# The order of gate and weight conversion in a two-layer feed-forward stage

## The chip, the cores and the metric

One core of a Trainium2 chip. The metric is the device time in microseconds (us) of one launch. "PE" is TensorE (matmuls; "PEld" its weight loads), "DVE" VectorE, "ACT" ScalarE, "POOL" GpSimd, "SP" the queue that issues the loads from memory.

## What is computed

Attention with a position bias for 2 x 8 heads of 576 tokens, whose output goes as 1152 rows of 512 through two feed-forward layers:

```python
attn_out = _attn_ref(**attn_kwargs)
x = np.ascontiguousarray(attn_out.transpose(0, 2, 1, 3)).reshape(B * S, H * D)
x = _moe_ref(x=x, **moe_kwargs)      # h = x @ w_in; g = h * sigmoid(1.702 h); g @ w_out
return _moe2_ref(x=x, **moe2_kwargs) # h = x @ w_in; g = P(h) / Q(h);          g @ w_out
```

Each layer has 512 inputs, 2048 hidden units and 512 outputs. Its weights `w_in` and `w_out` arrive in double precision.

## The kernel before, in words

**Stages.** Attention comes first, and its last steps overlap the start of the first layer (about 184 us into the span). Then follow the first layer (to about 390 us) and the second (to the end).

**Steps.** The hidden units are cut into 16 tiles of 128 ("f-tiles", `NF`), the 1152 rows into 3 chunks of 384 (`NC`, `CH`). A pair of a chunk and an f-tile is one step `n` of the main loop: 48 steps of the first layer (0 to 47, `N1 = 48`), then 48 of the second. The first layer takes f-tiles 0 to 7 for chunks 0, 1, 2 (steps 0 to 23), then f-tiles 8 to 15 for chunks 2, 1, 0 (steps 24 to 47). The second takes chunks 2, 1, 0 with all 16 f-tiles each. The first three steps are issued beside the end of attention, so the main loop begins with step 3.

**What a step issues**, each engine working through its own queue in the order of issue:

- PE, "hidden" (`hidden`, L476; matmuls at L483): 12 matmuls `w_in` times x into a PSUM tile `hps`. There are two such tiles, so hidden of step n needs the gate of step n-2 to have read its tile.
- The gate of the step before, n-1 (`gelu`, L498): ACT takes the sigmoid of `hps` into `sg` (L501), DVE multiplies `hps` and `sg` (L502), ACT rounds the product into `ghi` (L492), POOL subtracts to get the rest `glo` (L495). In the second layer the gate is `rational` (L509): it is spread over three steps, with ACT (L521 to L529), DVE (L531 to L545) and POOL (L542, L544). Its functions need another table on ACT, loaded once at step 48 (L899).
- PE, "out" (`out1`, L560, matmuls at L564; in the second layer `out2`, L567, at L571): the product of an earlier step (two steps back in the first layer, four in the second) times `w_out`, added up in PSUM. At the end of a run of f-tiles the sums are taken out (L819, L826, L848; the copies `xhi`, `xlo` of L831 and L832 follow one per step).

**Conversions.** A weight tile (`w_in` or `w_out` of one f-tile of one layer) is loaded as raw 64-bit numbers (`raw`, three buffers, L420) and turned into a rounded half and a rest. Conversion `j` does, in this order: on DVE it finishes conversion j-1 (`join`, L461), and begins its own with a shift into `top` (L446) and a merge (L451); on ACT it takes the lower word into `up` (L445), and casts the finished weights j-1 into the tile `w` (L471); POOL subtracts to get the rest of j-1 into `w` (L472); SP issues a load two conversions ahead. One set of 16 tiles `w` serves both layers, so a tile of the second layer can be written only when the first layer's last read of that f-tile is through. Which conversion comes is set by the list `M.order`; when, by the rules at L879 to L892 of the main loop: one per step, a second in the steps of the table `twice`, none before the old weights are freed, and from step 52 on one in every second step, where its DVE parts are put between those of `rational`.

**Order within a step, steps 6 to 48:** hidden, then the first conversion, then the gate, then the second conversion if there is one, then out. (Steps 3 to 5 have the gate ahead of both.)

**Conversions by step before:** one in each of steps 6 to 34; two in step 35; none in steps 36 to 40, since the next tile in the list is f-tile 8, which the first layer still reads; then 1, 1, 1, 2, 2, 2, 1 in steps 41 to 47; one in every even step from 52 to 64; the last `join` in step 66.

Of the kernel before, what the change touches and what calls it, by code (L numbers as in the profile page):

```python
# [17 lines left out]
NF = 16  # L18
# [4 lines left out]
L1, L2 = 2, 4  # L23
# [28 lines left out]
class Attention:  # L52
    def __init__(self, tc, t):
        self.tc, self.nc, self.t = tc, tc.nc, t
# [344 lines left out]
class Moe:  # L399
    def __init__(self, tc, t):  # L400
        self.tc, self.nc, self.t = tc, tc.nc, t
        self.raw, self.tmp, self.up, self.W = {}, {}, {}, {}
        self.hs, self.second = None, False
        self.ready = None
        self.order = [(0, k, o) for k in range(NF) for o in range(2)]
        self.order += [(1, k - L1 * o, o) for k in range(NF + L1) for o in range(2) if 0 <= k - L1 * o < NF]

# [165 lines left out]
def attention_moe_moe(tc, t):  # L575
    nc = tc.nc
    new = tc.alloc_tile_pool
    A, M = Attention(tc, t), Moe(tc, t)
# [33 lines left out]
    o = (1, 0, 3, 2, 5, 4, 7, 11, 6, 9, 8, 10)  # L612
# [42 lines left out]
    n = len(A.steps)  # L655
    nj = [0]

    def conv(now=True):
        M.conv(nj[0])
        nj[0] += 1  # L660
        if now:
            M.split()

    pv, hq, due = [], [], []
    A.pv = pv
    g, nh = {}, 0
    for s in range(n + TLAG + 2):
# [3 lines left out]
        if s < n:  # L671
            hp, b, qc = A.steps[s]
            pb = 2 * hp + b
            i = QORDER.index(qc)
# [77 lines left out]
        if s < n:  # L752
# [3 lines left out]
            if s:  # L756
                h, o, c = A.steps[s - 1]
# [46 lines left out]
    N1 = NC * NF  # L804
# [3 lines left out]
    freed = {k: max(due[n] - L1 for n in range(N1) if seq[n][2] == k) for k in range(NF)}  # L808
    acc, ng, later, hr = {}, len(g), [], []

    twice = (35, 37, 39, 40, 44, 45, 46)
    gq = list(range(N1, len(seq)))
    todo = list(range(len(seq)))

# [14 lines left out]
    def input2_parts():  # L829
        p, hi, lo = later.pop(0)  # L830
        nc.scalar.copy(hi, p)  # L831
        nc.gpsimd.tensor_tensor(out=lo, in0=p, in1=hi.bitcast(F32), op=ALU.subtract)  # L832
# [38 lines left out]
    for n in range(nh, len(seq) + L2):  # L871
        l, c, k = seq[n] if n < len(seq) else (2, 0, 0)
        M.second = l > 0
        if l < 2:
            (hr if l else hq).append(M.hidden(c, k))
        fs = []
        if n < 6:
            g[n - 1] = M.gelu(hq.pop(0))
        for i in range(2):  # L879
            j = nj[0]  # L880
            if j < 33:
                go = i == 0 or n < 6
            elif j < 65:
                go = freed[M.order[j - 1][1]] + L1 * M.order[j - 1][2] < n
                go = go and (n < N1 and (i == 0 or n in twice) or n >= N1 + 4 and n % 2 == 0 and i == 0)
            else:
                go = False
            if go and n >= N1:
                fs = M.convs(j)
                nj[0] += 1  # L890
            elif go:
                conv(False)  # L892
            if n < N1:
                M.split()
            if i == 0 and 6 <= n <= N1:
                g[n - 1] = M.gelu(hq.pop(0))

        if n == N1:
            nc.scalar.activation(out=small[:, 0:1], in_=small[:, 2:3], func=AF.Abs_reciprocal_sqrt)  # L899

        if n == N1 + 3:
            outs(n)
        if hr or n >= len(seq):
            r = M.rational(hr.pop(0) if hr else None, n < N1 + 4, fs)
            if r:
                g[gq.pop(0)] = r
        M.split()
        if later:
            input2_parts()
        if n != N1 + 3:  # L910
            outs(n)
# [74 lines left out]
```

## Time and profile before

| | |
|---|---|
| median of 3 runs | 605.54 us (605.29 to 606.39) |
| the profiled execution | 605.63 us, span 603.5 us |
| PE busy | 570.9 us (95% of the span) |
| ACT busy | 440.2 us (73%) |
| DVE busy | 427.4 us (71%) |
| POOL busy | 392.6 us (65%) |

The span runs from the first to the last instruction of the profiled execution; some 2 us of its time lie around it. The chain that ended last is PE for 63% of the span. Shares of busy time are an average over the stages: to see what a change is worth, one has to look at single steps.

### The profile page before, as it was taken

To read this page: it belongs to the slowest core of one execution; us is meant where nothing else is said; L and a number is where in the kernel's file an instruction comes from. 1 tells how busy PE (TensorE), PEld (TensorE's weight loads), DVE (VectorE), ACT (ScalarE), POOL (GpSimd) and SP (SyncE) were. 2 spreads that over 40 slices of the span, in tenths; PEclk is the share of its full clock that TensorE was granted. 3 is DMA by queue.
4 is the path that set the end of the run, shared out by engine and by line. 5 is a ranking of instruction groups with operands and counts; after the bars stand their busy time and mean duration, and the time that the engine had idled before them with its cause. 6 is when DMAs were issued, how large, how long until landed. Compare 5 with 4: busy or idle time off the path is not lost.

```text
span 603.5 us, 11022 instructions
## 1 busy us (share of the span) xinstructions
PE 570.9 (95%) x3805; PEld 477.7 (79%) x3805; DVE 427.4 (71%) x922; ACT 440.2 (73%) x927; POOL 392.6 (65%) x466
## 2 busy tenths in 40 slices
PE   6977999999889989999999999999999999999997
PEld 2233466666557989999999999988899899898995
DVE  7988756888876886657554527769899666667663
ACT  7977777898886675546454535679999978788783
POOL 5967666777764675546563536849888756566563
PEclk9999999999999999999999999999999999999999
DMA  5788762916314563525443313701210100001001
GB/s 175 209 269 277 225 233 83 317 60 229 113 36 140 175 209 118 163 78 168 138 111 101 105 36 105 210 1 35 72 35 2 52 2 1 1 15 38 2 1 52
DMA packets 23911, 66.25 MB, mean 110 GB/s; under 512 B 2480, under 2 KB 3376, under 8 KB 23856
## 3 DMA queue, kind: packets, MB, share of 16 engines
q1 hardware_dynamic: 23712, 65.43, 34.1%
q8 instruction: 30, 0.49, 0.3%
q14 instruction: 25, 0.20, 0.1%
q10 hardware_dynamic: 144, 0.13, 0.1%
HBM read 52.30 MB, written 13.25 MB: 109 GB/s over the span
## 4 chain that ended last, share of the span: by engine, by line
PE 63%; DVE 12%; ACT 11%; POOL 7%; issue 4%; DMA 3%; ACTq 0%; DVEq 0%; POOLq 0%
PE hps L483 23%; PE acc L564 12%; PE acc L571 11%; PE wide L215 5%; PE xt L370 3%; DVE p L236 3%; DMA bias_all<-st 2%; PE wide L122 2%; POOL ra L544 2%; POOL w L472 2%; DVE tmp L461 2%; PE pt L295 2%; PE pt L332 1%; POOL glo L495 1%; ACT w L471 1%
## 5 line engine op out<-in xcount | busy, mean ns | idle before, releaser
L483 PE MATMUL hps<-xhi,w 128*128 128x384 f32 x768 | 151.3, 338 | 3.4 <-DVE part L545 1.8
L483 PEld LDWEIGHTS hps<-xhi,w 128*128 128x128 f32 x768 | 135.5, 188 | 10.3 <-DVE part L545 3.9
L472 POOL TENSOR_TENSOR w<-tmp,w 128x512 fp32r<-128x512 f32 x64 | 85.9, 1342 | 36.3 <-ACT w L471 30.6
L495 POOL TENSOR_TENSOR glo<-sg,ghi 128x384 fp32r<-128x384 f32 x48 | 49.0, 1020 | 54.2 <-PE acc L564 40.6
L483 PE MATMUL hps<-xlo,w 128*128 128x384 f32 x384 | 82.0, 334 | 0.0
L253 POOL TENSOR_SCALAR p<-p,mn 128x512 f32<-128x512 f32 x72 | 55.4, 780 | 37.7 <-ACT p L240 26.2
L564 PE MATMUL acc<-ghi,w 128*128 128x384 f32 x384 | 78.3, 334 | 0.0
L571 PE MATMUL acc<-w,ghi 128*128 128x512 f32 x288 | 76.0, 393 | 1.1 <-POOL w L472 1.1
L240 ACT ACTIVATE p<-p,mn 128x576 f32<-128x576 f32 x72 | 55.4, 771 | 20.2 <-DVE mn L236 18.3
L483 PEld LDWEIGHTS hps<-xlo,w 128*128 128x128 f32 x384 | 68.0, 188 | 0.0
L564 PEld LDWEIGHTS acc<-ghi,w 128*128 128x128 f32 x384 | 67.6, 188 | 0.0
L542 POOL TENSOR_SCALAR ra<-ra,small 128x384 f32<-128x384 f32 x48 | 28.4, 592 | 53.2 <-ACT ra L527 53.1
L502 DVE TENSOR_TENSOR sg<-hps,sg 128x384 f32<-128x384 f32 x48 | 26.8, 558 | 50.6 <-ACT sg L501 50.6
L571 PEld LDWEIGHTS acc<-w,ghi 128*128 128x128 f32 x288 | 53.3, 188 | 10.0 <-POOL w L472 1.4
L236 DVE CUSTOM_DVE_ANT_0 p<-wide,bt 128x576 f32<-128x576 f32 x72 | 52.3, 750 | 2.3 <-DMA bt<-bias_all 2.1
L492 ACT CAST ghi<-sg 128x384 fp32r<-128x384 f32 x48 | 24.7, 514 | 39.4 <-PE acc L564 21.2
L544 POOL TENSOR_TENSOR ra<-ra,part 128x384 f32<-128x384 f32 x48 | 50.1, 1044 | 4.0
L445 ACT ACTIVATE up<-raw 128x512 int32<-128x512 uint32 x59 | 37.6, 637 | 19.1 <-DVE tmp L461 18.0
L215 PE MATMUL wide<-k,q 64*128 64x288 f32 (+1 forms) x432 | 45.2, 309 | 2.3 <-ACT st L142 2.0
L564 PE MATMUL acc<-glo,w 128*128 128x384 f32 x192 | 45.0, 334 | 0.0
L571 PE MATMUL acc<-w,glo 128*128 128x512 f32 x144 | 42.5, 392 | 0.0
L501 ACT ACTIVATE sg<-hps 128x384 f32<-128x384 f32 x48 | 23.5, 490 | 24.6 <-PE hps L483 24.6
(113 smaller groups left out, 1180.0 us busy)
## 6 DMA issues: line engine op xcount, KB each, us to landing
raw<-win SPq DMA_DIRECT2D x32, 512.0 KB, 3.5
raw<-wout SPq DMA_DIRECT2D x32, 512.0 KB, 3.5
bias_all<-st SPq DMA_DIRECT2D x36, 295.5 KB, 3.9
bt<-bias_all SPq DMA_DIRECT2D x16, 576.0 KB, 6.2
qk<-qk SPq DMA_DIRECT2D x7, 608.0 KB, 6.6
v<-v SPq DMA_DIRECT2D x8, 320.0 KB, 5.0
out<-o SPq DMA_DIRECT2D x8, 256.0 KB, 2.2
bt<-bias_all SPq DMA_DIRECT2D x8, 144.0 KB, 3.3
```

The costliest lines, as they stand in the source:

```text
L215: nc.tensor.matmul(ps[:, half, 0:288], q[p, x, 128 * qc:128 * qc + 128], k[p, y, 288 * half:288 * half + 288], start=(i == 0), stop=(i == ...
L236: nc.vector.tensor_tensor_reduce(out=pv.rearrange("p (x j) -> p x j", x=2), in0=ps[:, :, 0:288], in1=self.bt[qc][:, a, :].rearrange("p (x ...
L240: nc.scalar.activation(out=pv, in_=pv, func=AF.Exp, bias=mn[:, a:a + 1], scale=-1.0, accum_out=mn[:, 2 + a:3 + a])
L253: nc.gpsimd.tensor_scalar(out=p[:, a, 0:512], in0=p[:, a, 0:512], scalar1=r, scalar2=1.0, op0=ALU.mult, op1=ALU.mult)
L445: nc.scalar.activation(out=self.up[j].bitcast(I32), in_=lo, func=AF.Copy, scale=2.0 ** -29)
L472: nc.gpsimd.tensor_tensor(out=w[:, 2 * o + 1, :], in0=val, in1=w[:, 2 * o, :].bitcast(F32), op=ALU.subtract)
L483: nc.tensor.matmul(ps[:, 0:CH], w[:, wi, 128 * d:128 * d + 128], xx[:, d, :], start=(i == 0 and d == 0), stop=(i == 2 and d == 3))
L495: nc.gpsimd.tensor_tensor(out=glo[:], in0=g, in1=ghi[:].bitcast(F32), op=ALU.subtract)
L542: nc.gpsimd.tensor_scalar(out=t0[0][:], in0=t0[0][:], scalar1=self.pb[:, 1:2], scalar2=1.000001, op0=ALU.mult, op1=ALU.add)
L544: nc.gpsimd.tensor_tensor(out=t0[0][:], in0=t0[0][:], in1=t0[1][:], op=ALU.add)
L564: nc.tensor.matmul(acc[e][:, 0:CH], w[:, wi, 128 * e:128 * e + 128], g[gi][:], start=(first and i == 0), stop=(last and i == 2))
L571: nc.tensor.matmul(acc[e][:], g[gi][:, 128 * e:128 * e + 128], w[:, wi, :], start=(first and i == 0), stop=(last and i == 2))
```

## The change

The gate is issued ahead of the conversions in all steps of the first layer, no longer in steps 3 to 5 alone. The list of the second layer's tiles is cut in two: all of f-tiles 0 to 7 (`w_in` and `w_out`), then all of f-tiles 8 to 15; before, `w_in` of f-tiles 8 and 9 came ahead of `w_out` of 6 and 7. The table `twice` shrinks from seven steps to two.

```diff
@@ class Moe @@
-        self.order += [(1, k - L1 * o, o) for k in range(NF + L1) for o in range(2) if 0 <= k - L1 * o < NF]
+        for h in range(2):
+            ks = range(h * NF // 2, (h + 1) * NF // 2)
+            self.order += [(1, k - L1 * o, o) for k in range(ks[0], ks[-1] + 1 + L1) for o in range(2) if k - L1 * o in ks]
@@ attention_moe_moe @@
-    twice = (35, 37, 39, 40, 44, 45, 46)
+    twice = (44, 46)
...
-        if n < 6:
+        if n <= N1:
             g[n - 1] = M.gelu(hq.pop(0))
...
-            if i == 0 and 6 <= n <= N1:
-                g[n - 1] = M.gelu(hq.pop(0))
```

The lines of the program behind it stand two lines further down after the change (L502 becomes L504, and so on). PE's instructions and their order are the same. Three places show what moves.

ACT, steps 5 and 6, before: the gate of step 5, two conversions, and step 6, whose conversion stands ahead of its gate (`w_2733`, `w_2970` and `w_2971` are the weight tiles of f-tiles 6, 7 and 8):

```order
L501 ACTIVATE sg<-hps 128x384
L492 CAST ghi<-sg 128x384
L445 ACTIVATE up<-raw 128x512
L471 CAST w_2733<-tmp 128x512
L445 ACTIVATE up<-raw 128x512
L471 CAST w_2970<-tmp 128x512
L445 ACTIVATE up<-raw 128x512
L471 CAST w_2970<-tmp 128x512
L501 ACTIVATE sg<-hps 128x384
L492 CAST ghi<-sg 128x384
```

The same steps after the change:

```order
L503 ACTIVATE sg<-hps 128x384
L494 CAST ghi<-sg 128x384
L447 ACTIVATE up<-raw 128x512
L473 CAST w_2733<-tmp 128x512
L447 ACTIVATE up<-raw 128x512
L473 CAST w_2970<-tmp 128x512
L503 ACTIVATE sg<-hps 128x384
L494 CAST ghi<-sg 128x384
L447 ACTIVATE up<-raw 128x512
L473 CAST w_2970<-tmp 128x512
```

The gate issued in step 6 is two instructions further ahead on ACT; on DVE its product (L502, now L504) is ahead of the three instructions of the conversion in the same way.

ACT, from the conversions of step 46 to the table load of step 48, before (`w_2975` and `w_2973` are f-tiles 12 and 10):

```order
L445 ACTIVATE up<-raw 128x512
L471 CAST w_2975<-tmp 128x512
L445 ACTIVATE up<-raw 128x512
L471 CAST w_2973<-tmp 128x512
L501 ACTIVATE sg<-hps 128x384
L492 CAST ghi<-sg 128x384
L501 ACTIVATE sg<-hps 128x384
L492 CAST ghi<-sg 128x384
L899 ACT_TABLE_LOAD
```

After the change:

```order
L447 ACTIVATE up<-raw 128x512
L473 CAST w_2975<-tmp 128x512
L447 ACTIVATE up<-raw 128x512
L473 CAST w_2973<-tmp 128x512
L503 ACTIVATE sg<-hps 128x384
L494 CAST ghi<-sg 128x384
L447 ACTIVATE up<-raw 128x512
L473 CAST w_2976<-tmp 128x512
L503 ACTIVATE sg<-hps 128x384
L494 CAST ghi<-sg 128x384
L899 ACT_TABLE_LOAD
```

A further weight tile (`w_2976`, f-tile 13) is cast before step 48; the gate issued in step 47 stands ahead of that step's conversion.

POOL, steps 35 to 42, before (`glo` is the gate's rest, one per step; `w_2732`, `w_2733` are f-tiles 5 and 6):

```order
L472 TENSOR_TENSOR w_2970<-tmp,w_2970 128x512
L495 TENSOR_TENSOR glo<-sg,ghi 128x384
L472 TENSOR_TENSOR w_2732<-tmp,w_2732 128x512
L495 TENSOR_TENSOR glo<-sg,ghi 128x384 x5
L472 TENSOR_TENSOR w_2971<-tmp,w_2971 128x512
L495 TENSOR_TENSOR glo<-sg,ghi 128x384
L472 TENSOR_TENSOR w_2733<-tmp,w_2733 128x512
```

After the change:

```order
L474 TENSOR_TENSOR w_2970<-tmp,w_2970 128x512
L497 TENSOR_TENSOR glo<-sg,ghi 128x384
L474 TENSOR_TENSOR w_2732<-tmp,w_2732 128x512
L497 TENSOR_TENSOR glo<-sg,ghi 128x384
L474 TENSOR_TENSOR w_2733<-tmp,w_2733 128x512
L497 TENSOR_TENSOR glo<-sg,ghi 128x384
L474 TENSOR_TENSOR w_2970<-tmp,w_2970 128x512
L497 TENSOR_TENSOR glo<-sg,ghi 128x384 x3
L474 TENSOR_TENSOR w_2971<-tmp,w_2971 128x512
```

`w_out` of f-tiles 6 and 7 is finished in steps 37 and 38, ahead of the pause; before, they came after `w_in` of f-tile 8. In steps 35 to 38 there is now one conversion each, in steps 41 to 47 there are 1, 1, 1, 2, 1, 2, 1 (one fewer in all), and from step 52 on one in every even step up to 62, with the last `join` in step 64.

## Rows read from the trace of the kernel before

**Rows 1.** Busy time by stretch: stretch, its us, then each engine; PEclk; DMA.

```profile
340.00:360.00 20.00, 20.00 (x118) 20.00 (x117) 5.14 (x9) 6.32 (x13) 7.17 (x7) 1.00 0.17 54
400.00:420.00 20.00, 19.29 (x100) 17.43 (x99) 17.05 (x31) 17.23 (x38) 15.78 (x17) 1.00 0.08 27
```

**Rows 2.** Chain of waits, steps 12, 35 and 41: start, us, what.

```profile
241.60 2.08 PE acc L564 x12
...
335.21 2.38 PE hps L483 x12
...
363.45 1.95 DVE part L826 x4
```

**Rows 3.** Timeline, PE, steps 6 and 7: start, us, instructions [idle before <-releaser].

```profile
214.57 1.55 PE L564 MATMUL acc<-ghi,w 128*128 128x384 f32 x8
...
218.42 1.68 PE L483 MATMUL hps<-xhi,w 128*128 128x384 f32 x8 [1.61 <-DVE sg L502]
```

**Rows 4.** Timeline, ACT, DVE and POOL, steps 5 and 6.

```profile
214.56 0.61 ACT L471 CAST w<-tmp 128x512 fp32r<-128x512 f32 x1
...
214.67 0.69 DVE L451 SCALAR_TENSOR_TENSOR tmp<-raw,top 128x512 uint32<-128x512 uint32 x1
...
217.81 0.56 DVE L502 TENSOR_TENSOR sg<-hps,sg 128x384 f32<-128x384 f32 x1 [0.23 <-ACT sg L501]
...
215.25 1.29 POOL L472 TENSOR_TENSOR w<-tmp,w 128x512 fp32r<-128x512 f32 x1 [0.87 <-ACT w L471]
```

**Rows 5.** Timeline, DVE, gate products in steps 34, 35, 46 and 47.

```profile
334.60 0.56 DVE L502 TENSOR_TENSOR sg<-hps,sg 128x384 f32<-128x384 f32 x1 [0.28 <-ACT sg L501]
...
337.44 0.56 DVE L502 TENSOR_TENSOR sg<-hps,sg 128x384 f32<-128x384 f32 x1 [0.29 <-ACT sg L501]
...
383.96 0.56 DVE L502 TENSOR_TENSOR sg<-hps,sg 128x384 f32<-128x384 f32 x1 [0.23 <-ACT sg L501]
...
388.95 0.56 DVE L502 TENSOR_TENSOR sg<-hps,sg 128x384 f32<-128x384 f32 x1 [0.23 <-ACT sg L501]
```

**Rows 6.** Timeline, PE: hidden of steps 47, 48 (two rows), 53 and 60.

```profile
385.26 1.55 PE L483 MATMUL hps<-xhi,w 128*128 128x384 f32 x8
...
389.57 1.68 PE L483 MATMUL hps<-xhi,w 128*128 128x384 f32 x8
391.08 0.85 PE L483 MATMUL hps<-xlo,w 128*128 128x384 f32 x4
...
408.59 1.68 PE L483 MATMUL hps<-xhi,w 128*128 128x384 f32 x8 [0.71 <-DVE part L545]
...
438.90 1.57 PE L483 MATMUL hps<-xhi,w 128*128 128x384 f32 x8
```

**Rows 7.** Timeline, ACT, steps 48 and 51.

```profile
391.76 1.28 ACT L899 ACT_TABLE_LOAD   x1
...
393.17 0.47 ACT L527 ACTIVATE ra<-hps 128x384 f32<-128x384 f32 x1
...
405.36 0.50 ACT L525 ACTIVATE es<-part 128x384 f32<-128x384 f32 x1 [2.33 <-DVE part L531]
```

**Rows 8.** Timeline, PE: hidden of step 67, out within it, hidden of 68.

```profile
468.21 1.57 PE L483 MATMUL hps<-xhi,w 128*128 128x384 f32 x8
...
471.78 0.97 PE L571 MATMUL acc<-w,ghi 128*128 128x512 f32 x3 [1.06 <-POOL w L472]
...
473.73 1.57 PE L483 MATMUL hps<-xhi,w 128*128 128x384 f32 x8
```

**Rows 9.** Loads of raw weights on the page: count, KB, us to landing.

```profile
raw<-win SPq DMA_DIRECT2D x32, 512.0 KB, 3.5
```

**Rows 10.** Timeline, DVE merges in first and second layer; POOL beside the first.

```profile
222.51 0.69 DVE L451 SCALAR_TENSOR_TENSOR tmp<-raw,top 128x512 uint32<-128x512 uint32 x1
...
453.97 1.45 DVE L451 SCALAR_TENSOR_TENSOR tmp<-raw,tmp 128x512 uint32<-128x512 uint32 x1
...
221.91 1.02 POOL L495 TENSOR_TENSOR glo<-sg,ghi 128x384 fp32r<-128x384 f32 x1 [0.31 <-ACT ghi L492]
```

## The prediction

> **What bounds the kernel now.** I read the busy time by stretch first. Where the first layer runs steadily, PE is busy for 20.00 of 20 us while the other engines have two thirds of their time free; around the change of layers PE has gaps and DVE, ACT and POOL are near full [rows 1]. So the engines that convert and gate cost nothing in most steps, and a change to them pays only where PE waits. The chain of waits shows what a step costs when nothing is late: 2.08 us for hidden and 2.08 for out [rows 2]. I then went along PE's timeline for starts later than that. From 212 us to the end there are four places:
>
> - Step 7: hidden starts at 218.42, though out before it (from 214.57, 2.08 long) is through at 216.65. It waits for DVE's product L502, the last reader of its PSUM tile [rows 3].
> - Step 35: hidden takes 2.38 instead of 2.08 in the chain [rows 2], again behind L502, which ended at 335.16 [rows 5].
> - Steps 48 to 59: the change of layers, waiting for L502 and then for `rational` (DVE L545) [rows 6].
> - Step 67: out waits for POOL's L472, the rest of the last weight tile [rows 8].
>
> **Term 1, step 7: 1.90 us.** The late product belongs to the gate issued in step 6. Before, it stands behind the step's conversion: DVE ends the merge of step 5 at 214.67 + 0.69 = 215.36, but begins L502 only at 217.81 [rows 4]. Now ACT takes the sigmoid right behind the cast that ends at 214.56 + 0.61 = 215.17 [rows 4]. A sigmoid, taken to last as long as the square of the same shape, 0.47 [rows 7], ends by 215.7, and the product of 0.56 [rows 4] by 216.3, ahead of the 216.65 at which PE is ready. The rest of f-tile 7's `w_in`, which this hidden also reads, is done by POOL at 215.25 + 1.29 = 216.54 [rows 4], so it does not become the next wait. What goes: 218.42 - 216.65 = 1.77, and the 0.13 by which the first eight matmuls take longer after a stop (1.68 against 1.55) [rows 3]. Nothing hands it back soon after: what is put behind the gate is a conversion for f-tile 7's `w_out`, read two steps later, and weights for step 24 and beyond.
>
> **Term 2, step 35: 0.30 us.** L502 of step 34 moves ahead of one conversion. Term 1 shows what that is worth on DVE (217.81 - 215.36 = 2.45 us); only 0.30 is missing, so all of it goes. In the other steps up to 40 a gate that comes earlier gains nothing, as PE never waits there, and a conversion that comes later by a gate costs nothing either: its tile is read many steps on.
>
> **Term 3, the change of layers: 1.47 us.** ACT begins `rational` of step 48 at 393.17, right after the table load at 391.76 [rows 7]. Hidden of step 48 starts at 389.57, and its last four matmuls (from 391.08) end at 391.93 [rows 6]. Undisturbed it would start at 385.26 + 2 x 2.08 = 389.42 and, without the 0.13, end 0.28 earlier, at 391.65; with a handover of 0.05 (hidden of 7 began 0.05 after L502 ended, 218.42 against 217.81 + 0.56 [rows 3, 4]), ACT could begin at 391.70. That is 1.47 earlier. Is ACT free by then? The gate of step 47 needs hidden of 47 (385.26 + 2.08, so about 387.5), then half a microsecond each for sigmoid and product; its cast also waits until out of step 47 has read the old `ghi` (about 388.9), then some 0.5, then the load of 1.28 and a tiny operation: free at about 390.9, 0.8 to spare. DVE has to be there in time too. It leaves the sums of chunk 1 at 363.45 + 1.95 = 365.40 [rows 2], and from there works without a pause: a step with one conversion and a gate takes 337.44 - 334.60 = 2.84, one with two 388.95 - 383.96 = 4.99 [rows 5]. Before, steps 42 to 47 are three of each: 365.40 + 23.5 = 388.9, which is the L502 seen at 388.95. Now they are four and two: 386.7, over 1 us ahead of the product that waits for hidden of 47. So the chain that starts `rational` becomes PE's own. What follows goes hand to hand through the same engines (es at 405.36 waits 2.33 us for DVE; hidden of 53 waits for L545 [rows 6, 7]), so the 1.47 is carried through. Bounds: nothing, if the start of `rational` does not move; and all that PE loses from hidden of 47 to hidden of 60. That stretch took 438.90 - 385.26 = 53.64 us. It holds five hiddens and three outs of 2.08 (steps 47 to 51) and eight second-layer steps of 4.19 (seven of them took 468.21 - 438.90 = 29.31 [rows 6, 8]), 16.64 + 33.50 = 50.14, so 3.50 is lost. I take 1.47, since the engines stay the pace in steps 53 to 59, whose work is unchanged.
>
> **Term 4, step 67: 1.33 us.** Hidden of 67 to hidden of 68 takes 473.73 - 468.21 = 5.52 instead of 4.19, for L472 of the last tile [rows 8]. The last `join` moves from step 66 to step 64, two steps or 8.4 us earlier; 1.33 is missing.
>
> **Edits at no cost.** The three conversions now in steps 36 to 38 lie where DVE is busy for 5.14, ACT 6.32 and POOL 7.17 of 20 us [rows 1]; without that cover each would cost 4.99 - 2.84 = 2.15 on DVE's chain [rows 5]. Their loads go with them: a load is issued when the merge three conversions back frees its buffer and lands after 3.5 us [rows 9]; even in steps 44 to 47 two conversions and a gate lie between, some 5 us. SP's queue holds nothing else there. POOL's rest of the weights now queues behind `glo`, and `glo` behind PE's out; no first-layer reader is near.
>
> **The sum.** 1.90 + 0.30 + 1.47 + 1.33 = 5.00. The profiled execution took 605.63, so 600.63; it was 0.09 above the median of 605.54, so I predict **600.5 us**. A measurement here tells about 0.2%, 1.2 us, from no change.
>
> **Rivals.**
>
> *A. The gate holds up the conversions (602.0).* ACT's cast waits for DVE's product and for PE; with the gate first, the conversion stands behind that wait, and cannot begin before hidden of the step before is done. In steps 41 to 47 this could use up the microsecond that DVE has to spare, and `rational` would start as late as now: term 3 is nothing. For it: ACT and DVE show idle time before each product. Against: my count leaves more than 1 us. The Trainium skill (TensorE: Matmul & The Clock Gate, section "Architectural detail: the array is 16× 32×32, not 1× 128×128") says that ACT's and DVE's queues are strictly first-in first-out while PE's can pull weight loads ahead; by that rule the order of issue alone decides who waits, which speaks for A as for term 1.
>
> *B. Step 7 finds another wait (602.4).* The margins are 0.1 us for the weights and 0.4 for the product. If one of them, or a later gate, holds PE for as long, term 1 is nothing.
>
> *C. The whole loss at the change of layers goes (598.5).* If `rational` gets ahead far enough, steps 53 to 59 run at PE's pace: 3.50 instead of 1.47. Against: DVE, ACT and POOL are near full there [rows 1].
>
> *D. Slower (610.5).* `glo` on POOL now starts as the conversion starts on DVE. A merge takes 0.69 in the first layer and 1.45 in the second [rows 10]. If two of a conversion's three DVE instructions went to 1.45 in the eight conversions of steps 42 to 47, DVE would be 8 x 1.52 = 12.2 us later, less some 2.2 to spare on DVE and ACT: term 3 turns into a loss of about 8.5, against 3.5 from the other terms. It decides from about 0.9 us per conversion. Against: the merge at 222.51 runs beside `glo` (221.91 to 222.93) and takes 0.69 [rows 10]. The Trainium skill (SBUF — State Buffer, "Who interferes with whom") says that a DVE instruction with two SBUF inputs contends with a GpSimd instruction that reads SBUF, and one with a single SBUF input does not. By that rule D fails, as the first layer's merge has one input in PSUM (`top`), and the sum stays at 5.00; the trace agrees (0.69 and 1.45).
>
> *E. Nothing moves (605.5).* The lists of issue show that it does, so this is only for a fault in my reading.
>
> **Chances.** Forecast 0.66, A 0.12, B 0.08, C 0.08, D 0.03, E 0.03. All but D and E are faster by over 0.2%: 0.94; same 0.03, slower 0.03. The range of 598.9 to 602.5 takes in the forecast, A and B with what they may be off by; C lies just below it.
>
> **What would show it.** Step 7's hidden starts about 2.08 after out of step 6, with no idle; no idle before hidden of 35 and 48; ACT's first square of `rational` follows hidden of 48 by 0.05, with the table load ended before; hidden of 53 still shows a wait for DVE; out of step 67 shows none. I am wrong if PE idles in steps 8 to 46, or if a conversion waits for its load.

## The result and the profile after

The changed kernel takes 600.83 us (median of 4 runs, 600.31 to 601.84), beside 605.96 us (605.29 to 607.32, 4 runs) for the kernel before: a ratio of 0.9913 [95% interval 0.9898 to 0.9929]. That is 5.1 us less by the medians and 5.3 by the ratio (4.3 to 6.2). The forecast was 600.5 us, within 598.9 to 602.5. The profiled execution took 601.27 us, its span 599.4 against 603.5.

The page of the changed kernel: busy time, and the shares of the chain that ended last.

```profile
PE 571.2 (95%) x3805; PEld 479.1 (80%) x3805; DVE 426.2 (71%) x922; ACT 440.2 (73%) x927; POOL 390.1 (65%) x466
...
PE 76%; DVE 10%; ACT 5%; POOL 3%; issue 2%; DMA 2%; DVEq 0%; ACTq 0%; POOLq 0%
```

The engines are busy for nearly as long as before (POOL 390.1 against 392.6 us, the others closer); PE's share of the chain went from 63% to 76%. The work was moved, and waits went.

Busy time by stretch of the changed kernel (columns as in [rows 1]):

```profile
340.00:360.00 20.00, 20.00 (x117) 20.00 (x116) 8.23 (x14) 8.07 (x16) 8.04 (x8) 1.00 0.24 80
400.00:420.00 20.00, 19.30 (x98) 17.00 (x97) 17.70 (x32) 17.22 (x37) 16.60 (x18) 1.00 0.08 27
```

The two rows answer to [rows 1]. DVE, ACT and POOL took over conversions in the first, where PE still never stops. In the second PE is as before (19.30 against 19.29).

The timeline of PE in the changed kernel, steps 6 to 8, then hidden of 34, 36, 47, 48, 53, 60, 67 and 68 (columns as in [rows 3]):

```profile
213.43 1.55 PE L485 MATMUL hps<-xhi,w 128*128 128x384 f32 x8
...
215.51 1.55 PE L566 MATMUL acc<-ghi,w 128*128 128x384 f32 x8
...
217.59 1.55 PE L485 MATMUL hps<-xhi,w 128*128 128x384 f32 x8
...
221.75 1.55 PE L485 MATMUL hps<-xhi,w 128*128 128x384 f32 x8
...
329.91 1.55 PE L485 MATMUL hps<-xhi,w 128*128 128x384 f32 x8
...
338.23 1.55 PE L485 MATMUL hps<-xhi,w 128*128 128x384 f32 x8
...
383.99 1.55 PE L485 MATMUL hps<-xhi,w 128*128 128x384 f32 x8
...
388.15 1.55 PE L485 MATMUL hps<-xhi,w 128*128 128x384 f32 x8
...
405.86 1.68 PE L485 MATMUL hps<-xhi,w 128*128 128x384 f32 x8 [0.70 <-DVE part L547]
...
436.15 1.57 PE L485 MATMUL hps<-xhi,w 128*128 128x384 f32 x8
...
465.46 1.57 PE L485 MATMUL hps<-xhi,w 128*128 128x384 f32 x8
469.65 1.57 PE L485 MATMUL hps<-xhi,w 128*128 128x384 f32 x8
```

Before the change, hidden of 6, 8, 34 and 36 (the other starts stand in [rows 6] and [rows 8]):

```profile
212.49 1.55 PE L483 MATMUL hps<-xhi,w 128*128 128x384 f32 x8
...
222.72 1.55 PE L483 MATMUL hps<-xhi,w 128*128 128x384 f32 x8
...
330.88 1.55 PE L483 MATMUL hps<-xhi,w 128*128 128x384 f32 x8
...
339.50 1.55 PE L483 MATMUL hps<-xhi,w 128*128 128x384 f32 x8
```

Each term is the difference of one stretch between two starts of hidden, so it does not matter that stages ahead of it shift:

| term | stretch | before | after | gone | predicted |
|---|---|---|---|---|---|
| 1 | hidden 6 to 8 | 10.23 | 8.32 | 1.91 | 1.90 |
| 2 | hidden 34 to 36 | 8.62 | 8.32 | 0.30 | 0.30 |
| 3 | hidden 47 to 60 | 53.64 | 52.16 | 1.48 | 1.47 |
| 4 | hidden 67 to 68 | 5.52 | 4.19 | 1.33 | 1.33 |

Together 5.02 us, and nothing else moved: from hidden of step 3 to hidden of step 95, the last, PE takes 586.77 - 197.74 = 389.03 before and 582.69 - 198.68 = 384.01 after, again 5.02 less. The span shrank by 4.1 only, since in this execution the attention stage was longer: hidden of step 3 starts at 198.68, against 197.74 before, 0.94 later. The change does not touch that stage, and its length differs from execution to execution, together with TensorE's granted clock (the last section has the numbers).

Around the change of layers, the timeline of ACT in the changed kernel (gates of steps 45 and 47; the first square of `rational` last):

```profile
378.34 0.52 ACT L833 CAST xhi<-part 128x384 fp32r<-128x384 f32 x1
378.76 0.49 ACT L503 ACTIVATE sg<-hps 128x384 f32<-128x384 f32 x1
...
386.11 0.60 ACT L473 CAST w<-tmp 128x512 fp32r<-128x512 f32 x1
386.62 0.48 ACT L503 ACTIVATE sg<-hps 128x384 f32<-128x384 f32 x1
...
388.33 1.28 ACT L899 ACT_TABLE_LOAD   x1
...
390.43 0.49 ACT L529 ACTIVATE ra<-hps 128x384 f32<-128x384 f32 x1 [0.60 <-PE hps L485]
```

The square now waits 0.60 us for PE, where before it stood right behind the table load [rows 7]. From hidden of 47 it starts 390.43 - 383.99 = 6.44 later, before 393.17 - 385.26 = 7.91 [rows 6, 7].

The gate products on DVE, same kernel, gates of steps 42 to 47:

```profile
367.36 0.56 DVE L504 TENSOR_TENSOR sg<-hps,sg 128x384 f32<-128x384 f32 x1 [0.84 <-ACT sg L503]
...
370.60 0.56 DVE L504 TENSOR_TENSOR sg<-hps,sg 128x384 f32<-128x384 f32 x1 [0.70 <-ACT sg L503]
...
376.02 0.56 DVE L504 TENSOR_TENSOR sg<-hps,sg 128x384 f32<-128x384 f32 x1 [0.65 <-ACT sg L503]
...
379.28 0.56 DVE L504 TENSOR_TENSOR sg<-hps,sg 128x384 f32<-128x384 f32 x1 [0.70 <-ACT sg L503]
...
384.29 0.56 DVE L504 TENSOR_TENSOR sg<-hps,sg 128x384 f32<-128x384 f32 x1 [0.24 <-ACT sg L503]
...
387.13 0.56 DVE L504 TENSOR_TENSOR sg<-hps,sg 128x384 f32<-128x384 f32 x1 [0.29 <-ACT sg L503]
```

From product to product, a step with one conversion takes 3.24 and 3.26 us (3.31 for the one ahead of these rows, from 364.05) and 2.84 in the last; one with two takes 5.42 and 5.01. The shorter of each kind are those after the last copy `xhi`, which ACT casts between the conversion and the sigmoid (378.34 to 378.76, a place of 0.42). I had counted 2.84 and 4.99 for all of them.

### The profile page after: what moved, and what is told of

Same layout as the page of the kernel before. It is cut to its first block, busy times and chain, and to the rows that moved or that the text cites. A ratio compares the mean times of both kernels' runs of the same rounds, so it can differ in the third digit from the quotient of the medians.

```text
span 599.4 us, 11018 instructions
## 1 busy us (share of the span) xinstructions
PE 571.2 (95%) x3805; PEld 479.1 (80%) x3805; DVE 426.2 (71%) x922; ACT 440.2 (73%) x927; POOL 390.1 (65%) x466
## 4 chain that ended last, share of the span: by engine, by line
PE 76%; DVE 10%; ACT 5%; POOL 3%; issue 2%; DMA 2%; DVEq 0%; ACTq 0%; POOLq 0%
PE hps L485 30%; PE acc L566 16%; PE acc L573 15%; PE wide L215 5%; DVE p L236 3%; PE xt L370 3%; DMA bias_all<-st 2%; PE pt L295 2%; PE wide L122 1%; PE pt L332 1%; DVE room L103 1%; ACT p L240 1%; PE xt L373 1%; POOL room L98 1%; PE narrow L122 1%
## 5 line engine op out<-in xcount | busy, mean ns | idle before, releaser
L504 DVE TENSOR_TENSOR sg<-hps,sg 128x384 f32<-128x384 f32 x48 | 26.7, 557 | 52.1 <-ACT sg L503 52.1
```

## The experiments

The theory: terms 1 and 2 come from the gate's place alone, term 3 from the table `twice`, term 4 from the list, and they add up. The first rival: the gate's place is worth something at the change of layers too, so that the parts don't divide like this. The kernel before was run again beside each group of experiments; the time behind "against" is its median there. These ratios have intervals of about 1 us to either side, so the terms are told apart by the stretches between two starts of hidden.

**1. The gate alone** (old list and table, gate ahead; the edit is shown against the changed kernel, as in all experiments):

```diff
-        for h in range(2):
-            ks = range(h * NF // 2, (h + 1) * NF // 2)
-            self.order += [(1, k - L1 * o, o) for k in range(ks[0], ks[-1] + 1 + L1) for o in range(2) if k - L1 * o in ks]
+        self.order += [(1, k - L1 * o, o) for k in range(NF + L1) for o in range(2) if 0 <= k - L1 * o < NF]
...
-    twice = (44, 46)
+    twice = (35, 37, 39, 40, 44, 45, 46)
```

> Only the gate's place is changed (gate ahead of the conversions in steps 6 to 48); the old list of tiles and the old table of double steps stay. My theory: terms 1 (1.90 us, step 7) and 2 (0.30, step 35) are the gate's and come in full; term 4 (1.33, step 67) stays lost, since the last join is still in step 66. Term 3 needs a thinner conversion load: with three double steps in a row DVE reaches the product before step 48 some 1.75 us later than in the changed kernel, whose ACT had 0.60 to spare before rational, so 1.15 of 1.47 is lost and 0.3 comes. Sum 2.5 us faster than before, 603.3 us or so. Rival: the place of the gate alone frees ACT for rational and gives all of term 3: 3.7 us faster, 602.2.

604.54 us against 606.81, ratio 0.9962 [0.9948, 0.9976]: 2.3 us gone. Hidden 6 to 8 and hidden 34 to 36 take 8.32 each, so terms 1 and 2 are there in full. At the change of layers nothing was gained, though hidden of 48 is on time (4.16 after hidden of 47, 4.31 before): 47 to 60 takes 53.62. And 67 to 68 takes 5.52. ACT's timeline in this kernel:

```profile
391.95 1.28 ACT L897 ACT_TABLE_LOAD   x1
...
393.35 0.47 ACT L527 ACTIVATE ra<-hps 128x384 f32<-128x384 f32 x1
```

The square is again right behind the table load, 393.35 - 385.45 = 7.90 after hidden of 47. The 0.3 that I had given to the gate there did not come, and the rival falls.

**2. The order alone** (new list and table, gate behind the conversion):

```diff
-        if n <= N1:
+        if n < 6:
             g[n - 1] = M.gelu(hq.pop(0))
...
+            if i == 0 and 6 <= n <= N1:
+                g[n - 1] = M.gelu(hq.pop(0))
```

> Only the list of tiles and the table of double steps are changed; the gate stays behind the first conversion in steps 6 to 48. My theory: terms 1 and 2 do not come (hidden of step 7 still idles some 1.6 us, hidden of 35 is some 0.3 late); term 4 comes in full (1.33); term 3 comes in full or nearly (1.4), since four single and two double steps leave DVE and ACT free before hidden of 48 ends. Sum 2.8 us faster than before, 603.0 us or so. Rival (term 3 is the gate's place): only term 4, 1.3 us faster, 604.5.

603.89 us against 606.81, ratio 0.9951 [0.9936, 0.9967]: 3.0 us gone. 47 to 60 takes 52.15 and 67 to 68 takes 4.18; hidden 6 to 8 takes 10.21 and 34 to 36 takes 8.61. The PE row of step 7 and the ACT row of the first square, from the timeline of this kernel:

```profile
220.88 1.66 PE L485 MATMUL hps<-xhi,w 128*128 128x384 f32 x8 [1.61 <-DVE sg L504]
...
394.11 0.49 ACT L529 ACTIVATE ra<-hps 128x384 f32<-128x384 f32 x1 [0.36 <-PE hps L485]
```

The wait of [rows 3] is back to the hundredth, while the square waits for PE (6.43 after hidden of 47, at 387.68). The two halves, 2.3 and 3.0 by the ratios, add up to the 5.3 of the whole; by the stretches they are 2.21 and 2.83, together 5.04.

**3. The list with the old table** (gate ahead), to part term 3 from term 4:

```diff
-    twice = (44, 46)
+    twice = (35, 37, 39, 40, 44, 45, 46)
```

> The changed kernel with the old table of double steps: gate ahead and the new list, but two conversions in steps 35, 44, 45 and 46. My theory: the new list alone gives term 4 (the last join is then in step 62), the gate's place terms 1 and 2, and the third double step takes term 3 away: rational's first square follows the start of hidden of 47 by 7.9 us as before and not by 6.44. 3.5 us faster than before, 1.5 slower than the changed kernel. Rival: the list gives term 3 too (fewer conversions of f-tiles 8 to 15 are left after the pause): 5.0 us faster than before.

602.76 us against 606.26, ratio 0.9942 [0.9929, 0.9954]: 3.5 us gone. 67 to 68 takes 4.19, while 47 to 60 takes 53.64, as before. ACT's timeline in this kernel:

```profile
389.81 1.28 ACT L899 ACT_TABLE_LOAD   x1
...
391.22 0.47 ACT L529 ACTIVATE ra<-hps 128x384 f32<-128x384 f32 x1
```

So term 3 needs the one conversion fewer in steps 41 to 47, and the list without it gives term 4 alone. The new table with the old list was not run, so whether the table gives term 3 without the list stays open.

**4. A doubled merge**, to price rival D and the spare time of the conversions: the eight conversions of steps 42 to 47 write the same merged value twice.

```diff
+        self.again = range(50, 58)
...
             def merge():
-                nc.vector.scalar_tensor_tensor(out=val[:], in0=hi, scalar=0xC0000000, in1=self.tmp[j][1],
-                                               op0=ALU.bitwise_and, op1=ALU.bitwise_or)
+                for _ in range(2 if j in self.again else 1):
+                    nc.vector.scalar_tensor_tensor(out=val[:], in0=hi, scalar=0xC0000000, in1=self.tmp[j][1],
+                                                   op0=ALU.bitwise_and, op1=ALU.bitwise_or)
```

> The changed kernel, with DVE's merge (L453) issued twice in the eight conversions of steps 42 to 47 (the second writes the same again). My theory: DVE's queue in steps 42 to 47 sets when rational can start, with little to spare. Each single step then takes 3.6 instead of about 3.25 us and each double 6.5 instead of about 5.2, together 4.3 us more, of which ACT's 0.60 of idle time before rational takes up a part: the first square of rational starts about 3.7 us later relative to hidden of 46, and the kernel is 3.7 us slower than the changed one, about 604.5. Rival: rational's start is PE's alone and DVE has room: same time as the changed kernel, 600.8.

603.42 us against 606.81, ratio 0.9949 [0.9931, 0.9966]. Slower than the changed kernel, but by less than expected: the first square starts 393.40 - 385.49 = 7.91 after hidden of 47, 1.47 later than in the changed kernel, and 47 to 60 takes 53.61, 1.45 more. DVE's timeline in this kernel shows why:

```profile
376.90 1.41 DVE L455 SCALAR_TENSOR_TENSOR tmp<-raw,top 128x512 uint32<-128x512 uint32 x2
378.24 0.56 DVE L506 TENSOR_TENSOR sg<-hps,sg 128x384 f32<-128x384 f32 x1
...
381.49 0.56 DVE L506 TENSOR_TENSOR sg<-hps,sg 128x384 f32<-128x384 f32 x1
...
387.63 0.55 DVE L506 TENSOR_TENSOR sg<-hps,sg 128x384 f32<-128x384 f32 x1
...
390.81 0.55 DVE L506 TENSOR_TENSOR sg<-hps,sg 128x384 f32<-128x384 f32 x1
```

The products no longer wait. The two merges take 1.41 where one took 0.69. A step with one conversion and a copy still takes 3.25 (378.24 to 381.49): the second merge filled the 0.70 for which DVE had waited there. Only the step without a copy (3.18 instead of 2.84) and the doubles grew, to 6.14 from 5.42 and 5.01. So in the steps with a copy DVE's own work did not set the pace; each product had waited for ACT's sigmoid. The product of 47's gate came 390.81 - 385.49 = 5.32 after hidden of 47, against 387.13 - 383.99 = 3.14; 2.18 less the spare 0.60 is 1.58, and 1.47 arrived at the square.

**5. Copies later**: the copies of chunk 0 (`xhi`, `xlo`), which lie in steps 52 to 55, go to steps 60 to 63.

```diff
-        if later:
+        if later and (n < N1 or n >= N1 + 12):
             input2_parts()
```

> The changed kernel, with the four copies of chunk 0's sums (ACT L833, POOL L834, 1.02 us each on POOL) issued in steps 60 to 63 instead of 52 to 55; they are read in step 80. My theory: POOL and ACT are what paces steps 53 to 57, with these copies beside the conversions, so the 0.98 us that PE still loses from hidden of 53 to hidden of 60 (30.29 instead of 29.31) mostly goes, and the wait of hidden 53 for DVE (0.70) stays: 0.6 to 1.0 us faster than the changed kernel, about 600.0. Rival: the conversions in steps 52, 54 and 56 pace these steps: no change.

600.19 us against 606.81, ratio 0.9894 [0.9877, 0.9911]. PE's timeline, hidden of 53 and 60:

```profile
405.80 1.66 PE L485 MATMUL hps<-xhi,w 128*128 128x384 f32 x8 [0.73 <-DVE part L547]
...
435.27 1.57 PE L485 MATMUL hps<-xhi,w 128*128 128x384 f32 x8
```

These seven steps take 29.47 instead of the 30.29 of the changed kernel, close to the undisturbed 29.31; hidden of 53 waits as before (0.73 against 0.70). By itself this looked like my picture of steps 53 to 59: engines that are full, and pace PE.

**6. The sums behind the product**: what hidden of 53 waits for, followed back. In step 51 DVE takes chunk 0's sums out (L828) ahead of the `rational` product L533. ACT's `es` waits for that product, which reads the PSUM tile that `es` is written to. This kernel issues the sums behind the product.

```diff
-    def rational(self, h, early, fs):
+    def rational(self, h, early, fs, mid=None):
...
             vec.scalar_tensor_tensor(out=t2[2][:], in0=sq, scalar=0.75, in1=t2[2][:], op0=ALU.add, op1=ALU.mult)
+        if mid:
+            mid()
...
-        if n == N1 + 3:
-            outs(n)
         if hr or n >= len(seq):
-            r = M.rational(hr.pop(0) if hr else None, n < N1 + 4, fs)
+            r = M.rational(hr.pop(0) if hr else None, n < N1 + 4, fs, (lambda: outs(n)) if n == N1 + 3 else None)
```

> The changed kernel; in step 51 the sums of chunk 0 (DVE L828, 1.94 us in four instructions) are issued one instruction later, behind DVE's product L533 on which ACT's es waits (2.33 us). My theory: the wait of hidden 53 (0.70 idle, 1.0 in all) is these sums in front of L533; es then starts some 1.5 us earlier, hidden of 53 waits for nothing or nearly, and 0.8 to 1.0 us go at that place; but steps 54 to 59 stay paced by POOL and ACT, whose work starts about 1.0 earlier as well, so that it is carried through: 599.9. Rival: out of step 52 then waits for the sums to leave PSUM, and nothing is gained: 600.8.

598.94 us against 606.26, ratio 0.9878 [0.9865, 0.9892]: faster than both kernels, and by more than expected. 47 to 60 takes 50.31, 1.85 less than in the changed kernel and 0.17 above the 50.14 of a stretch without any wait. First the timeline of the changed kernel in step 51, DVE and ACT:

```profile
400.13 1.94 DVE L828 TENSOR_TENSOR part<-acc,part 128x384 f32<-128x384 f32 x4
401.99 0.55 DVE L533 SCALAR_TENSOR_TENSOR part<-sq,part 128x384 f32<-128x384 f32 x1
...
402.63 0.49 ACT L527 ACTIVATE es<-part 128x384 f32<-128x384 f32 x1 [2.33 <-DVE part L533]
```

The same step in this kernel (the sums are L830), with PE's hidden of 53 and 60:

```profile
399.31 0.55 DVE L533 SCALAR_TENSOR_TENSOR part<-sq,part 128x384 f32<-128x384 f32 x1
399.78 1.94 DVE L830 TENSOR_TENSOR part<-acc,part 128x384 f32<-128x384 f32 x4
...
399.96 0.50 ACT L527 ACTIVATE es<-part 128x384 f32<-128x384 f32 x1 [0.47 <-DVE part L533]
...
404.14 1.57 PE L485 MATMUL hps<-xhi,w 128*128 128x384 f32 x8
...
433.49 1.57 PE L485 MATMUL hps<-xhi,w 128*128 128x384 f32 x8
```

Busy time by stretch of this kernel:

```profile
400.00:420.00 20.00, 20.00 (x103) 18.21 (x102) 19.10 (x34) 19.52 (x42) 18.27 (x20) 1.00 0.16 52
```

`es` waits 0.47 instead of 2.33, and PE does not stop in the stretch, though the copies are still there. DVE, ACT and POOL do more in the same 20 us (19.10, 19.52 and 18.27 against 17.70, 17.22 and 16.60): what had looked like full engines was a chain that had fallen behind by the sums and, with the copies in its way, did not catch up.

**7. Both of the last two:**

> The changed kernel with both: the copies of chunk 0 in steps 60 to 63, and the sums of step 51 behind L533. My theory: the two gains add up, 0.8 (measured for the copies) and 0.9: from hidden of 47 to hidden of 60 PE takes 50.3 instead of 52.16 us, next to the 50.14 of an undisturbed run; 1.7 us faster than the changed kernel. Rival: without the copies POOL catches up anyway, and the second gain is only partly new: 1.0 us faster.

598.83 us against 606.26, ratio 0.9887 [0.987, 0.9903]; 47 to 60 takes 50.28. That is the stretch expected, but nothing beyond kernel 6 alone (50.31): the 0.82 of the copies is part of its 1.85. The copies cost PE something only while the chain is late.

**8. The gate ahead in few steps**, to see whether the others matter: steps 3 to 6 and 34 only.

```diff
-        if n <= N1:
+        ahead = n <= 6 or n == 34
+        if ahead:
             g[n - 1] = M.gelu(hq.pop(0))
...
+            if i == 0 and not ahead and n <= N1:
+                g[n - 1] = M.gelu(hq.pop(0))
```

> The changed kernel, but with the gate ahead of the conversions in steps 3 to 6 and 34 alone; in the other 41 steps it stands behind the first conversion as before. My theory: all that the gate's place gives comes from the gates issued in steps 6 and 34 (terms 1 and 2), and the rest of the gain is the list's and the table's: same time as the changed kernel, with hidden of 7 and of 35 on time and rational's first square 6.44 us after the start of hidden of 47. Rival: the place of the gate in steps 41 to 47 has a part in term 3: up to 1.5 us slower than the changed kernel.

601.59 us against 606.26, ratio 0.9928 [0.9914, 0.9941]. PE's timeline, steps 7 to 9:

```profile
216.52 1.55 PE L485 MATMUL hps<-xhi,w 128*128 128x384 f32 x8
...
221.08 1.66 PE L485 MATMUL hps<-xhi,w 128*128 128x384 f32 x8 [0.24 <-DVE sg L504]
...
225.36 1.55 PE L485 MATMUL hps<-xhi,w 128*128 128x384 f32 x8
```

Hidden of 7 is on time and hidden of 8 is not: 216.52 to 225.36 is 8.84 instead of 8.32, so 0.5 of term 1 is lost again, one step later. 34 to 36 takes 8.32, and 47 to 60 takes 52.16: term 3 in full, with the gate behind the conversion from 35 on.

**9. One step more** (`n <= 7 or n == 34`), beside the changed kernel once more on the same chip:

> As the run with the gate ahead in steps 3 to 6 and 34, but in step 7 too. That run showed the wait at step 8 instead of step 7 (hidden 8 was 0.5 late, for DVE's product). My theory: one step more and DVE has caught up, so that hidden of 7, 8 and 35 are all on time, and the kernel takes as long as the changed one (beside it here), although 40 of the 43 steps have the old order. Rival: the wait moves on to step 9 with another 0.3 to 0.5 us.

> The changed kernel itself, on the same chip, for comparison: about 5 us faster than before.

601.22 us (600.28 to 602.92) and 601.39 us (600.87 to 602.85), against 606.36, ratios 0.9922 [0.9908, 0.9937] and 0.9923 [0.9911, 0.9935]: the same. From hidden of 3 to hidden of 95 they take 384.03 and 384.01. With the gate ahead up to step 7, hidden of 7, 8 and 9 start 4.16 apart. So of some forty gates that the change moves, the ones issued in steps 6, 7 and 34 carry all of its gain from the gate.

## Why the prediction was right, and where its steps were not

The signs that the prediction named came: hidden of 7 starts 2.08 behind out of step 6 (217.59 - 215.51), hidden of 36 and 48 show no loss, the first square waits for PE behind the table load, hidden of 53 still waits 0.70 for DVE, and PE does not idle in steps 8 to 46.

**What bounds the kernel.** The stretch from 340 to 360 us, from which I read that the other engines have two thirds of their time free, holds the steps without a conversion. From 240 to 260 us, where each step has one, DVE was busy for 12.51, ACT for 10.81 and POOL for 12.12 of 20 us before the change. No term rests on the two thirds.

**Term 1 (1.90, measured 1.91).** Right, with its working. ACT's sigmoid, DVE's product and POOL's rest of the weights in the changed kernel:

```profile
216.03 0.49 ACT L503 ACTIVATE sg<-hps 128x384 f32<-128x384 f32 x1
...
216.55 0.56 DVE L504 TENSOR_TENSOR sg<-hps,sg 128x384 f32<-128x384 f32 x1 [0.24 <-ACT sg L503]
...
216.20 1.29 POOL L474 TENSOR_TENSOR w<-tmp,w 128x512 fp32r<-128x512 f32 x1 [0.88 <-ACT w L473]
```

The changed kernel runs 213.43 - 212.49 = 0.94 later here; without that, the sigmoid ends at 215.58 (predicted 215.7), the product at 216.17 (216.3), POOL's rest of the weights at 216.55 (216.54), and PE is ready at 216.65. The margins were 0.48 and 0.10; the latter is all that kept rival B (step 7 finds another wait) away. The 0.13 that PE loses behind a stop was rightly part of the term: without it the sum would be 1.77. What I did not see is that step 7's gate is needed too: experiment 8, without it, lost 0.5 in step 8. Rival B named a later gate as a possible wait, and only the gate's place in step 7 kept it away. The order of issue alone moved this wait there and back (experiments 1 and 2). The Trainium skill (TensorE: Matmul & The Clock Gate, "Architectural detail: the array is 16× 32×32, not 1× 128×128") calls ACT's and DVE's queues strictly first-in first-out; the trace agrees (idle of 1.61 with the gate behind, none with the gate ahead).

**Term 2 (0.30, measured 0.30).** Right, by experiments 1 and 2; step 34's gate alone suffices (experiment 8).

**Term 3 (1.47, measured 1.48).** The size is right and its cause too: the list and the table without the gate give it (experiment 2), the gate without them does not (1), and the list with the old table does not either (3). Two steps of its working are wrong.

- DVE "from there works without a pause: a step with one conversion and a gate takes 337.44 - 334.60 = 2.84". DVE did pause. The rows that gave 2.84 [rows 5] lie at step 35, where no copy `xhi` runs. In steps 42 to 45 ACT casts one ahead of each sigmoid, and the steps are 0.4 longer. From the first product after the sums (364.05) to the end of the last conversion (386.15 + 0.69 = 386.84) four singles and two doubles took 22.79, where I had 4 x 2.84 + 2 x 4.99 = 21.34. The 1.45 came out of the microsecond and more that I thought DVE had: the sigmoid of 47 stands right behind the cast of 386.11, with hidden of 47 done at 383.99 + 2.08 = 386.07. I had checked the count on the steps before (388.9 counted, 388.95 seen), but there a shorter first step (2.35 from the sums to the first product) hid two longer ones of 3.10. ACT's own margin, which I gave as 0.8, was 0.60, and that held. So the count was wrong, and the term came in full because of what was left to spare; in experiment 4 more work on DVE used that up, and the 1.47 was gone.
- "I take 1.47, since the engines stay the pace in steps 53 to 59, whose work is unchanged." The reason is wrong, by experiment 6: with the same work in them, those steps run at PE's 4.19 once the sums of step 51 stand behind L533. The row that shows it was among mine, `es` waiting 2.33 us for DVE [rows 7]. I took it for the engines being full and did not ask what DVE did in that time: 1.9 us of sums. My argument against rival C was the busy share of [rows 1], and that was no evidence. For the forecast it made no difference, because the change leaves the sums where they are.

**Term 4 (1.33, measured 1.33).** Right: the list, by experiment 3, which has it, against experiment 1, which does not.

**The rivals.** A (the gate holds up the conversions): steps 42 to 47 did run longer than counted, but the order of gate and conversion is not to blame. With the gate behind (experiment 8) the square waits 0.35 for PE, with the gate ahead 0.60; the place of the gate cost nothing here. C did not come with this change, but 1.85 of the 2.02 us that the changed kernel still loses there can be had. D (slower): no merge of the first layer got longer. All 53 that have `top` in PSUM took 0.69 in the changed kernel, and the one at 218.41 ran beside a `glo` from 217.81 to 218.83. The Trainium skill (SBUF — State Buffer, "Who interferes with whom") says that a DVE instruction with at most one SBUF input, outside the 2-port perf modes, does not contend with GpSimd; the trace agrees (0.69). What the 1.45 of the second layer owes to contention is not shown: those merges (1.37 to 1.46 in the changed kernel) all ran beside a POOL instruction. D's price was too high as well: by its sum, 0.72 more per conversion would cost 8 x 0.72 - 2.2 = 3.6 us at the start of `rational`, and it cost 1.47 (experiment 4), since much of it fell into waits for ACT. The 1.52 per conversion of D itself was not run.

## What to carry to other kernels

A product that frees a PSUM tile belongs ahead of the conversions in the queues, but it pays only in the few steps where PE really waits for it: find those by PE's late starts, not by busy shares. A step that several in-order engines share must be timed on a step that holds the same instructions on all of them; one short cast on another engine made most of mine 0.4 us longer. And where a row says that one engine waits 2 us for another, look up what the other does in those 2 us before calling it full: here four additions in front of one product cost 1.85 us, and moving them behind it brought the time down to 598.94 us.

## What was not expected of the hardware

- A chain across ACT, DVE and POOL that falls behind by 1.9 us can go on costing PE time for seven steps, though each engine is below 90% busy (17.70, 17.22 and 16.60 of 20 us): from hidden of 53 to hidden of 60 PE lost 0.98 us more. Without the copies in those steps it lost 0.16 (experiment 5). Once on time, the chain keeps PE's pace at 18.27 to 19.52 of 20, copies and all.
- The attention stage differs by up to 2.6 us between executions of kernels that do the same there, and TensorE's granted clock differs with it. Hidden of step 3 starts at 197.74 in the profiled execution before, at 198.68 after and at 200.14 in experiment 1, and from 40 to 80 us the mean granted clock was 1.00, 0.94 and 0.87 of full speed. In all twelve profiled executions the order is the same: clocks of 0.96 to 1.00 go with starts up to 198.0, 0.94 with 198.6 to 198.8, 0.87 to 0.91 with 200.1 to 200.2. That the clock causes the longer stage is not shown. A single span can't show effects of 1 us; stretches between two marks behind that stage repeat to some hundredths (hidden 6 to 8 takes 8.32 in nine executions of eight kernels).
